# A fixed attention order, wider sums, copied up tiles, five shared PSUM banks and a last tile in halves, in an attention and gated-MLP kernel

## The chip, the cores and the metric

The kernel runs on one core of a Trainium2 chip. The metric is device time in microseconds (us) of one execution; lower is better. "Span" is the time from the first to the last instruction in the trace of one profiled execution, 1.7 to 2.9 us less than the time reported for the same execution.

Engines in the profile: PE is TensorE, PEld its weight loads, DVE is VectorE, ACT is ScalarE, POOL is GpSimd, SP is SyncE; a "q" behind a name is the engine's issuing of DMA transfers.

## The reference

Layer norm of x (2048 rows of 512), then a sliding, dilated attention (32 heads of 16, 8 keys at a distance of 2), times a silu gate from a GELU-gated MLP of width 1792, plus x. All in bfloat16.

```python
def _A_ref(x, wqkv, wo):                      # H = 32, Dh = 16, W = 8, dil = 2
    q, k, v = ...                             # x @ wqkv, by heads
    idx = pos[:, None] - arange(W)[None, :] * dil
    logits = einsum("bhsd,bhswd->bhsw", q, k[idx]) * Dh ** -0.5   # masked where idx < 0
    attn = softmax(logits)
    return einsum("bhsw,bhswd->bhsd", attn, v[idx]) @ wo

def _B_ref(x, w_gate, w_up, w_down):
    return (gelu(x @ w_gate) * (x @ w_up)) @ w_down

xn = layernorm(x)
return x + _A_ref(xn, wqkv, wo) * silu(_B_ref(xn, w_gate, w_up, w_down))
```

## The kernel before

The rows are handled in four blocks of 512. For a block, TensorE makes q, k and v; VectorE multiplies q by shifted k (a "product", 128x2048) and adds pairs of products; TensorE sums over the 16 elements of a head with 32-column matmuls ("logits sum", L_ps); ScalarE takes exp; TensorE sums the weights of the eight keys (sum_ps), VectorE takes the reciprocal (rs), TensorE spreads it back to 128 partitions (b_ps) and ScalarE copies it out (b_sb). Then VectorE multiplies the weights by the values and TensorE sums again ("value sums", O_ps). Gate and up matmuls (g_ps, u_ps) and the output tiles (y_ps, s_ps) fill TensorE's time around this.

The program doesn't write its instructions in the order of the code. Every step is a task with an estimated duration, and a planner simulates the engines and writes each engine's instructions in the order of the simulated starts. Each engine then runs its own list strictly in that order.

```python
MM = 0.216          # the planner's durations, us
PROD = 1.14         # a 128x2048 product or pair addition on VectorE
HMUL = 0.6
ACT1 = 0.62
HOP = 0.2
# ... class Order, in run():
    for t in left:
        s = self.ready(t)              # engine free, inputs done, buffer free
        k = (round(s, 3), t.prio, t.seq)
        if best is None or k < best[0]:
            best = (k, t, s)
```

PSUM has eight banks here: four for q/k/v, gate, up and output tiles, two for the small attention tiles and transposes, and one tile of two banks for the value sums.

```python
psf = pool("psf", 4, space=bass.MemoryType.PSUM)
psa = pool("psa", 2, space=bass.MemoryType.PSUM)
pso = pool("pso", 1, space=bass.MemoryType.PSUM)
```

The logits are summed in two halves of four keys each, eight matmuls a half.

```python
def reduce(w2=w2, prods=prods):
    L = psa.tile([P, TQ], F32, name="L_ps", tag="a")
    for i in range(2):
        for w4 in range(4):
            nc.tensor.matmul(L[32 * w4 : 32 * (w4 + 1), :], lhsT=quad[:],
                             rhs=prods[2 * i][:, w4, :], start=(i == 0), stop=(i == 1))
# ...
s = add("pe", 0.4, sums, deps=[(e, 0.3) for e in exps], prio=-0.4, takes=[("a", ("sum", j))])
r = add("dve", 1.15, recip, deps=[s], prio=-1.5, frees=[("a", ("sum", j))])
b = add("pe", 0.3, spread_back, deps=[r], prio=-0.4, takes=[("a", ("b", j))])
b_ready[j] = add("act", ACT1, b_copy, deps=[b], prio=-0.6, frees=[("a", ("b", j))])
```

The large weights are loaded from ScalarE's list of instructions:

```python
def start(o, i, dep):
    add("act", 0.5, load(o, i), deps=[dep], prio=-3.0)      # load: nc.scalar.dma_start
start(wg_sb[:], ..., copied[2])
start(wu_sb[:], ..., k_ready[1])
for e in range(4):
    start(wo_sb[32 * e : 32 * (e + 1), :, :], v[e], k_ready[2])
start(wd_sb[:], ..., q_ready[3])
```

The last output tile gates its first 384 columns, then the other 128 (`edges = (0, D - P, D)`), behind one silu over all 512.

The softmax here doesn't subtract the row's maximum and nothing guards it: scores larger than these inputs give would overflow.

## Time and profile before

| | before |
|---|---|
| time, median of 6 runs | 230.94 us (230.4 to 231.9) |
| span of the profiled run | 229.0 us |
| first projection matmul | 7.69 us |
| end of the last matmul to the end | 4.4 us |
| VectorE busy | 193.4 us |
| ScalarE busy | 111.1 us |

Between the first and the last matmul TensorE runs at 0.216 us for every 128x512 matmul, with few gaps. Its lines are shown and read in the prediction below.

In a timeline line the columns are: start, duration of the group, engine, source line, operation, output<-input, number of instructions; in brackets the engine's idle time before it and what ended it. Records of a few matmuls can be missing from a trace. A step between the starts of two matmuls that is exactly twice the usual one is such a hole and not a wait, so I read waits from starts together with their releasers. The size of a TensorE wait is the step between two starts less the usual one; that is up to 0.2 us more than the bracket, which starts counting at a modelled end.

### The profile page before, as it was taken

How to read it: one execution, taken by the hardware profiler on the slowest of the kernel's cores; microseconds unless marked ns; L12 is line 12 of the kernel's file. 1: busy time of each engine (PE TensorE's matmuls, PEld its weight loads, DVE VectorE, ACT ScalarE, POOL GpSimd, SP SyncE). 2: the span in 40 equal slices, each digit the busy share in tenths (PEclk: the TensorE clock that was granted, in tenths of full speed). 3: DMA queues.
4: the chain of work that ended last, by engine and by line, in shares of the span. 5: the costliest groups of instructions: out<-in, count | busy, mean ns of one | idle time of the engine just before them, and what ended most of it. 6: DMA issues, size and time to landing. Idle time of an engine off the chain costs nothing.

```text
span 229.0 us, 3272 instructions
## 1 busy us (share of the span) xinstructions
PE 222.1 (97%) x1234; PEld 104.8 (46%) x1234; DVE 193.4 (84%) x270; ACT 111.1 (49%) x167; POOL 28.3 (12%) x67
## 2 busy tenths in 40 slices
PE   7899999999999999999999999999999999999992
PEld 2796554354444444444444444444444344444441
DVE  4899999999999999999999999999759997342322
ACT  3576568477634365464445374434563164334211
POOL 7102930400412000040400002100000000000000
PEclk9999999999999999999999999999999999999999
DMA  5994799599718000054520011900000100000010
GB/s 172 342 384 163 166 207 375 163 296 336 185 32 186 3 0 23 23 141 94 134 54 3 0 46 28 207 0 0 1 3 23 46 24 0 3 0 0 23 46 25
DMA packets 15072, 22.64 MB, mean 99 GB/s; under 512 B 1472, under 2 KB 11984, under 8 KB 15056
## 3 DMA queue, kind: packets, MB, share of 16 engines
q0 software_dynamic: 2592, 8.54, 16.8%
q1 hardware_dynamic: 8592, 7.57, 10.5%
q10 hardware_dynamic: 3872, 6.32, 7.8%
q8 instruction: 9, 0.15, 0.3%
q14 instruction: 7, 0.06, 0.1%
HBM read 18.22 MB, written 4.21 MB: 98 GB/s over the span
## 4 chain that ended last, share of the span: by engine, by line
PE 88%; DMA 9%; DVE 1%; SPq 0%; ACT 0%; ACTq 0%; issue 0%; DVEq 0%
PE g_ps L710 21%; PE u_ps L710 21%; PE y_ps L764 21%; PE qkv_ps L430 12%; DMA wu_sb<-in_B_w_up_dram 7%; PE s_ps L752 6%; DMA wqkv_sb<-in_A_wqkv_dram 3%; PE O_ps L656 2%; PE L_ps L534 1%; PE tr_ps L351 1%; PE sum_ps L588 0%; PE b_ps L606 0%; SPq L196 0%; DVE sg L778 0%; ACT vst L454 0%; DVE sg L785 0%
## 5 line engine op out<-in xcount | busy, mean ns | idle before, releaser
L710 PE MATMUL g_ps<-xnT,wg_sb 128*128 128x512 bf16 x224 | 57.6, 380 | 0.0
L710 PE MATMUL u_ps<-xnT,wu_sb 128*128 128x512 bf16 x224 | 57.6, 380 | 0.0
L720 ACT ACTIVATE gl<-g_ps 128x512 bf16<-128x512 f32 x56 | 33.4, 597 | 48.8 <-PE g_ps L710 48.7
L764 PE MATMUL y_ps<-wd_sb,hT 128*128 128x512 bf16 x224 | 51.3, 380 | 0.0
L727 DVE TENSOR_TENSOR hT<-gl,u_ps 128x512 bf16<-128x512 bf16 x56 | 38.0, 683 | 12.5 <-PE u_ps L710 12.4
L430 PE MATMUL qkv_ps<-xnT,wqkv_sb 128*128 128x512 bf16 (+1 forms) x240 | 43.9, 337 | 1.1 <-DMA wqkv_sb<-in_A_wqkv_dram 0.6
L639 DVE TENSOR_TENSOR pv<-attn,v_arr 128x2048 bf16<-128x2048 bf16 x32 | 38.4, 1219 | 0.1
L517 DVE TENSOR_TENSOR prod<-q_sb,k_sb 128x2048 bf16<-128x2048 bf16 x32 | 38.3, 1219 | 0.0
L710 PEld LDWEIGHTS <-wg_sb 128*128 128x128 bf16 x224 | 21.4, 98 | 27.6 <-issue 2.5
L710 PEld LDWEIGHTS <-wu_sb 128*128 128x128 bf16 x224 | 21.6, 98 | 27.2 <-issue 1.7
L764 PEld LDWEIGHTS <-hT 128*128 128x128 bf16 x224 | 21.5, 98 | 25.7 <-issue 0.4
L430 PEld LDWEIGHTS <-wqkv_sb 128*128 128x128 bf16 x240 | 24.9, 108 | 16.5 <-issue 1.3
L496 POOL DMA_DIRECT2D v_arr<-vT_dram x32 | 18.7, 590 | 100.9 <-DVE pv L639 86.7
L775 ACT ACTIVATE sil<-y_ps 128x512 bf16<-128x512 f32 x16 | 9.6, 597 | 33.2 <-PE y_ps L764 33.1
L778 DVE TENSOR_TENSOR sg<-sil,s_ps 128x512 bf16<-128x512 bf16 (+2 forms) x17 | 11.1, 653 | 11.5 <-PE s_ps L752 7.7
L527 DVE TENSOR_TENSOR prod<-prod 128x2048 bf16<-128x2048 bf16 x16 | 19.5, 1221 | 0.2
L649 DVE TENSOR_TENSOR pv<-pv 128x2048 bf16<-128x2048 bf16 x16 | 19.5, 1220 | 0.2
L752 PE MATMUL s_ps<-wo_sb,o_sb 128*128 128x512 bf16 (+2 forms) x68 | 16.5, 367 | 0.0
L303 DVE BATCH_NORM_STATS2 stats<-x_sb 128x6 f32<-128x512 bf16 x16 | 10.8, 673 | 2.0 <-DMA x_sb<-in_A_x_dram 2.0
L454 ACT ACTIVATE vst<-qkv_ps 128x512 bf16<-128x512 f32 x16 | 9.4, 600 | 6.3 <-PE qkv_ps L430 3.1
L443 ACT ACTIVATE q_sb<-qkv_ps 128x512 bf16<-128x512 f32 x16 | 9.5, 604 | 4.8 <-PE qkv_ps L430 4.8
L449 ACT ACTIVATE k_sb<-qkv_ps 128x512 bf16<-128x512 f32 x16 | 9.2, 598 | 3.9 <-PE qkv_ps L430 3.9
(56 smaller groups left out, 121.1 us busy)
## 6 DMA issues: line engine op xcount, KB each, us to landing
v_arr<-vT_dram POOLq DMA_DIRECT2D x32, 260.0 KB, 5.2
vT_dram<-vst SPq DMA_DIRECT2D x16, 128.0 KB, 6.0
out_dram<-sg SPq DMA_DIRECT2D x15, 128.0 KB, 1.7
wg_sb<-in_B_w_gate_dram ACTq DMA_DIRECT2D x1, 1792.0 KB, 9.3
wu_sb<-in_B_w_up_dram ACTq DMA_DIRECT2D x1, 1792.0 KB, 15.0
wd_sb<-in_B_w_down_dram ACTq DMA_DIRECT2D x1, 1792.0 KB, 10.0
wqkv_sb<-in_A_wqkv_dram SPq DMA_DIRECT2D x3, 512.0 KB, 6.9
x_sb<-in_A_x_dram SPq DMA_DIRECT2D x2, 512.0 KB, 8.9
```

The source lines that it names most:

```text
L430: nc.tensor.matmul(ps[:, i * n : (i + 1) * n], lhsT=wqkv_sb[:, which, ws], rhs=xnT[:, dk, j * TQ + lo : j * TQ + lo + n], start=(dk == 0), ...
L496: nc.gpsimd.dma_start(out=v_arr[32 * w4 : 32 * (w4 + 1), :, :], in_=src)
L517: nc.vector.tensor_tensor(out=prod[:], in0=tiles["q", j][:, c, :].unsqueeze(1).to_broadcast([P, 4, TQ]), in1=kwin, op=ALU.mult,)
L527: nc.vector.tensor_tensor(out=a[:], in0=a[:], in1=b[:], op=ALU.add)
L639: nc.vector.tensor_tensor(out=pv[:], in0=tiles["attn", j][:, w2, :].unsqueeze(1).to_broadcast([P, 4, TQ]), in1=tiles["va", j, half][:, 4 * ...
L649: nc.vector.tensor_tensor(out=a[:], in0=a[:], in1=b[:], op=ALU.add)
L710: nc.tensor.matmul(ps[:], lhsT=w[:, dk, fc * P : (fc + 1) * P], rhs=xnT[:, dk, j * TQ : (j + 1) * TQ], start=(dk == 0), stop=(dk == NC - 1),)
L720: nc.scalar.activation(out=tiles["gl", j, fc][:], in_=tiles["g_ps", j, fc][:], func=AF.Gelu_apprx_tanh)
L727: nc.vector.tensor_tensor(out=tiles["h", j][:, fc, :], in0=tiles["gl", j, fc][:], in1=tiles["u_ps", j, fc][:], op=ALU.mult,)
L752: nc.tensor.matmul(tiles["s", t][:, cs], lhsT=tiles["o", j][:, c, tt * P : (tt + 1) * P], rhs=wo_sb[:, c, cs], start=(c == 0), stop=(c == ...
L764: nc.tensor.matmul(tiles["y", t][:], lhsT=tiles["h", j][:, fc, tt * P : (tt + 1) * P], rhs=wd_sb[:, fc, :], start=(fc == 0), stop=(fc == N ...
L778: nc.vector.tensor_tensor(out=tiles["sg", t][:, cs], in0=tiles["sil", t][:, cs], in1=tiles["s", t][:, cs], op=ALU.mult,)
```

## The change

The intent: give VectorE less to do and TensorE fewer reasons to wait. In its parts:

- The attention batches have a fixed order on VectorE, with the logits of block j+1 ahead of the values of block j.
- The two halves of the logits are summed in one group of 16 matmuls, with one exp over 1024 columns.
- In blocks 0 and 1, ScalarE copies each up tile out of PSUM, so VectorE multiplies from SBUF.
- The query weights come in four loads, on two queues, ahead of the other weights.
- Five PSUM banks are shared by transposes, projections, gate, up and output tiles; one is left for the small attention tiles.
- The last output tile has its y matmuls, silu, gate, addition and store in two halves of 256 columns.
- The products and their sums, which shared six SBUF buffers, get two and five of their own; the normalised inputs get three buffers in place of four.

```diff
+BATCHES = [
+    ("S", 0), ("S", 1), ("V", 0, 0), ("V", 0, 1), ("S", 2), ("V", 1, 0), ("V", 1, 1),
+    ("S", 3), ("V", 2, 0), ("V", 2, 1), ("V", 3, 0), ("V", 3, 1),
+]
+UP_BY_ACT = [(j, fc) for j in range(2) for fc in range(14)]
 ...
-    psf = pool("psf", 4, space=bass.MemoryType.PSUM)
-    psa = pool("psa", 2, space=bass.MemoryType.PSUM)
+    psf = pool("psf", 5, space=bass.MemoryType.PSUM)
+    psa = pool("psa", 1, space=bass.MemoryType.PSUM)
 ...
+    for k in range(NC):
+        eng = nc.sync if k % 2 == 0 else nc.scalar
+        eng.dma_start(
+            out=wqkv_sb[:, 0, k * D : (k + 1) * D], in_=A_wqkv[k * P : (k + 1) * P, 0:D]
+        )
 ...
-    load_wqkv(0)
     load_wqkv(1)
 ...
+    chain = [None]
+    def add_vector(dur, fn, deps, **kw):
+        chain[0] = add("dve", dur, fn, deps=[*deps, chain[0]], prio=1.0, **kw)
+        return chain[0]
 ...
+    def scores_sum(j):
+        L = pso.tile([P, 2, TQ], F32, name="L_ps", tag="o")
+        for w2 in range(2):
+            for i in (1,) if j in FULL else (0, 1):
+                for w4 in range(4):
+                    nc.tensor.matmul(
+                        L[32 * w4 : 32 * (w4 + 1), w2, :], lhsT=quad[:],
+                        rhs=results[("S", j), 2 * w2 + i][:, w4, :],
+                        start=(i == 0 or j in FULL), stop=(i == 1),
                     )
 ...
+        def evacuate():
+            nc.scalar.activation(out=hidden(), in_=tiles["u_ps", j, fc][:], func=AF.Copy)
 ...
-        edges = (0, D) if not split else (0, D - P, D)
-        columns = [slice(a, b) for a, b in zip(edges, edges[1:])]
+        columns = [slice(0, D // 2), slice(D // 2, D)] if split else [slice(0, D)]
 ...
+            ys = [add_y(cs) for cs in columns]
+            ss = add_s()
 ...
+    for batch in BATCHES:
+        attention_batch(*batch)
```

## The prediction

> **What bounds the kernel now.** I read the page first (parts 1, 2 and 4), then busy time by stage, then the order of time at the few places where TensorE loses something.
>
> ```profile
> PE 222.1 (97%) x1234; PEld 104.8 (46%) x1234; DVE 193.4 (84%) x270; ACT 111.1 (49%) x167; POOL 28.3 (12%) x67
> PE   7899999999999999999999999999999999999992
> ...
> PE 88%; DMA 9%; DVE 1%; SPq 0%; ACT 0%; ACTq 0%; issue 0%; DVEq 0%
> ```
>
> PE is busy in every slice but the first and the last. Busy is not yet full speed, so I checked the spacing: in the chain, four 128x512 matmuls take 0.86 us, 0.216 us each. From the first projection matmul (7.68 us) to the end of the last (224.67 us) the stream runs at that spacing; the starts in the trace show 3 to 4 us of larger steps in all. So the time is 7.7 us of start, 217 us of matmuls and 4.4 us of tail, and only what shortens one of the three can help. By stage (the columns are PE, PEld, DVE, ACT, POOL):
>
> ```profile
> 55.64:81.60 25.96, 25.96 (x137) 10.95 (x135) 25.93 (x30) 12.84 (x19) 4.62 (x8) 1.00 0.47 108
> ...
> 209.00:224.67 15.67, 15.65 (x77) 7.18 (x75) 4.02 (x7) 3.56 (x5) 0.00 (x0) 1.00 0.07 25
> 224.67:229.04 4.37, 0.00 (x0) 0.00 (x0) 1.34 (x4) 0.00 (x0) 0.00 (x0) 0.87 0.11 32
> ```
>
> In the first block of gate and up matmuls (first line) VectorE is as full as PE and ScalarE is half empty. Still PE doesn't wait: VectorE keeps up just in time, so relieving it gives no time by itself.
>
> Three places do lose time. First, the column-tiled sums:
>
> ```profile
> 58.07 1.03 PE L710 MATMUL u_ps<-xnT,wu_sb 128*128 128x512 bf16 x4
> 59.02 0.62 PE L656 MATMUL O_ps<-pv,fold 128*32 128x512 bf16 x8
> 59.57 1.04 PE L710 MATMUL g_ps<-xnT,wg_sb 128*128 128x512 bf16 x4
> ```
>
> The next gate matmul would have begun at 58.07 + 4 x 0.216 = 58.93 and begins at 59.57: eight 32-column matmuls cost 0.64 us, two passes of 0.216 (four run side by side) and 0.20 to switch over and back.
>
> Second, a stall at 43 us, where ScalarE stands still for 3 us while it issues loads and waits, so that the four PSUM banks fill:
>
> ```profile
> 42.80 0.62 PE L534 MATMUL L_ps<-prod,quad 128*32 128x512 bf16 x8
> 43.25 1.08 ACT L454 ACTIVATE vst<-qkv_ps 128x512 bf16<-128x512 f32 x2 [3.08 <-DMA wu_sb<-in_B_w_up_dram]
> 43.90 1.89 PE L430 MATMUL qkv_ps<-xnT,wqkv_sb 128*128 128x512 bf16 x8 [0.48 <-ACT vst L454]
> ```
>
> Third, the two ends:
>
> ```profile
> 6.76 0.43 DVE L361 COPY xnT<-tr_ps 128x512 bf16<-128x512 bf16 x1 [0.49 <-PE tr_ps L351]
> 7.68 2.81 PE L430 MATMUL qkv_ps<-xnT,wqkv_sb 128*128 128x256 bf16 x24 [0.63 <-DMA wqkv_sb<-in_A_wqkv_dram]
> ...
> 223.61 1.04 PE L752 MATMUL s_ps<-wo_sb,o_sb 128*128 128x384 bf16 x8
> 223.81 0.60 ACT L775 ACTIVATE sil<-y_ps 128x512 bf16<-128x512 f32 x1 [3.29 <-PE y_ps L764]
> 224.74 0.56 DVE L778 TENSOR_TENSOR sg<-sil,s_ps 128x384 bf16<-128x384 bf16 x1 [2.75 <-PE s_ps L752]
> ```
>
> The transposed input is there at 7.19, the query weights only at 7.65. At the end the gate on the first 384 columns does not start when their four matmuls are done (about 224.4, and silu is done at 224.41) but after all eight, at 224.74: the program orders accesses to one PSUM bank as a whole.
>
> **What the Trainium skill says.** "TensorE: Matmul & The Clock Gate", section "Back-to-back issue gap", gives N/2.4 + 2.5 ns, 216 ns for 512 columns: the trace has 0.216, so the stream is at its floor. "VectorE: DVE Perf Modes", "The perf-mode tier table", has tensor_tensor at half rate when an operand is in PSUM: the trace agrees, 683 ns for hT (u in PSUM) against 424 for the residual add (both in SBUF). "ScalarE: Activation LUTs", "What ACT_TABLE_LOAD costs", gives about 1283 ns; the trace has 1283. "PSUM — Partial Sum Buffer", "PSUM bank collisions raise a hardware error", tells to guard PSUM by bank, not by address; the late gate above is that rule at work.
>
> **The change part by part.**
> - *Logits sums.* The 64 matmuls stay, but come as 4 groups of 16 in place of 8 of 8: 0.20 + 4 x 0.216 = 1.06 us against 2 x 0.64 = 1.28. Gain 4 x 0.2 = 0.8 us, all on the path. The value sums are unchanged.
> - *Query weights in four loads on two queues, ahead of the others.* The first matmul can begin just after 7.19, 0.4 us earlier. But the value weights landed at 3.27 + 8.2 = 11.5 us (issue plus the longest of their three landing times) and are first used at 11.65; they leave a little later now, so part of it is waited for again. I count 0.3.
> - *Five shared banks in place of four.* One bank more holds 0.86 us of matmuls, more than the 0.5 us stall at 43 us. Gain 0.5, if transposes, which now use the same banks, don't take it.
> - *Up tiles of blocks 0 and 1 copied by ScalarE.* VectorE saves 28 x (0.683 - 0.41) = 7.6 us, none on the path. ScalarE gets 28 x 0.60 = 16.8 us. In the first block it holds 12.8 us in 26; with 14 x 0.6 = 8.4 more, and exp of block 1, which now falls here with two more table loads (1.0 + 2 x 1.28 = 3.6), it is near 24 to 25 of 27. Just enough on average, but exp between two table loads keeps ScalarE from both PSUM tiles for 3.6 us, in which PE fills 3.6 / 0.86 = 4.2 banks of five; the gelu table load just before adds 1.28. So a short stall can appear here: 0 to 1 us.
> - *Fixed order, logits a block ahead.* Values of block j now come last before its output tiles. In the kernel before, both logits of block 1 and the values of block 0 were done by 79.6 us, so the amount needed by then is the same 36 products and sums, but half a logits batch of slack is gone. The 3.8 us that VectorE saves per block replaces it. I count 0.3 us, with a tail to 2.
> - *Last tile in halves.* PE work is the same (28 x 0.109 against 14 x 0.216). Silu of half 0 is placed between the first and second seven matmuls of half 1. Both halves lie in one bank, so by the bank rule that silu waits for those seven, and the next seven wait for silu. Matmul to ScalarE about 0.3, silu on 256 columns about 0.385 (from 597 for 512 and 1023 for 1024), and back: an estimated 0.65 us stall. The VectorE end is no shorter: gates and residuals of 256 columns, interpolated from those of 128, 384 and 512, are 2 x (0.42 + 0.29) = 1.42 us, before 0.56 + 0.36 + 0.28 + 0.23 = 1.43. Loss 0.6.
>
> Sum: -0.8 - 0.3 - 0.5 + 0.6, and new stalls of 0.5 = -0.5 us, 230.4.
>
> **The rivals.** (a) *The order works as meant and no new stall appears*, and the halves don't hold each other up: 230.9 - 1.6 = 229.3. For it: VectorE is 100% busy in the middle now, and more slack lets buffers free earlier. Against: PE doesn't wait for it even now. (b) *ScalarE becomes the bound of blocks 0 and 1*: each exp costs PE 1 to 1.5 us, and the hidden tiles come late at the output tiles: 232 to 233. For it: 24 to 25 of 27 us. Against: exp of blocks 2 and 3 can fall among output tiles, where ScalarE is idle about half the time, and four wide exps in place of eight save table loads. (c) *PE waits for the value sums before each block's output tiles*, as the order was fixed with durations for VectorE some 7% shorter than the trace has (1.14 against 1.22): 2 us at up to three blocks, 235. Against: the same shortfall in the kernel before left no PE stall.
>
> **Range and chances.** Even with all gains and no stall the time is near 229, so 2% (226.3) is out of reach unless the PE stream itself shrinks. 2% slower (235.5) takes 5 us of new stalls, rival (c) in full. The range covers rival (a) and most of (b).
>
> **What would show it.** PE's waits: none at 43 us; logits sums in 4 runs of 16 of about 1.1 us; the first projection matmul near 7.3; ScalarE above 85% in the first gate/up block; in the last tile a gap of about 0.6 us between the seventh and eighth matmul of the second half, released by silu; VectorE near 186 us busy. Wrong, if PE waits on value sums at the output tiles or on up-tile copies for more than 2 us, or if the start moves by over 1 us.

## The result, and the profile after

| | before | after |
|---|---|---|
| median of 6 runs, us | 230.94 | 233.01 |
| lowest to highest, us | 230.4 to 231.9 | 232.47 to 233.24 |
| span of the profiled run, us | 229.0 | 231.1 |
| VectorE busy, us | 193.4 | 187.7 |
| ScalarE busy, us | 111.1 | 121.8 |

The ratio of after to before is 1.0081, with a 95% interval of 1.0055 to 1.0107: within 2%, so "same" by that measure, but the interval excludes 1. Ratios here and below are, to within 0.0005, the mean time of one kernel's runs over the mean of the runs of the kernel before from the same rounds, so not quite the ratio of the medians quoted. Executions over 1.5% slower than the fastest of the same kernel are left out of the means. I predicted a gain of 0.5 us; the kernel lost 2.1 us. The 233.01 lies 0.4 us above the range of 228.8 to 232.6.

The page of the changed kernel, parts 1, 2 and 4:

```profile
PE 220.5 (95%) x1224; PEld 106.9 (46%) x1246; DVE 187.7 (81%) x269; ACT 121.8 (53%) x189; POOL 27.8 (12%) x67
...
PE   7999999898999999999999999999999999999991
...
PE 75%; DMA 11%; DVE 8%; ACT 2%; issue 1%; SPq 0%; ACTq 0%; DVEq 0%
```

VectorE has less to do, as meant, and PE has two slices below 90% in the middle, where it had none. The chain that ended last gives the reading: before, it was PE for 88% and VectorE for 1%; now VectorE holds 8% and ScalarE 2%. So TensorE waits for them somewhere. (22 of 1246 matmul records are missing here, so PE's busy time can't be compared to a microsecond.)

The first block of gate and up matmuls, and the time after the last matmul, by stage (window, length, then busy time and instructions of PE, PEld, DVE, ACT, POOL; then the clock, the DMA share and GB/s):

```profile
55.89:83.58 27.69, 27.13 (x155) 11.55 (x157) 27.48 (x36) 22.87 (x35) 4.62 (x8) 1.00 0.46 110
226.29:231.10 4.81, 0.00 (x0) 0.00 (x0) 1.34 (x4) 0.00 (x0) 0.00 (x0) 1.00 0.10 29
```

ScalarE is busy 22.87 of 27.69 us, 83%, where it was half empty. VectorE is as full as before: the window is 1.73 us longer, and with shorter multiplications of the up tiles it holds 20 products and pair additions where it held 17, and block 1's reciprocal. The tail takes 4.81 us in place of 4.37.

The start, in order of time:

```profile
7.34 2.78 PE L446 MATMUL qkv_ps<-xnT,wqkv_sb 128*128 128x256 bf16 x24 [0.28 <-DVE xnT L377]
...
11.69 1.48 PE L446 MATMUL qkv_ps<-xnT,wqkv_sb 128*128 128x256 bf16 x12 [0.24 <-DMA wqkv_sb<-in_A_wqkv_dram]
```

The first projection matmul starts at 7.34, released by the transposed input and no longer by a load. It comes 0.35 us earlier. But at 11.69 TensorE stands still for the value weights; by the starts, 0.41 us are lost there. The early start is given back whole.

Around 43 us, and the softmax scaling of block 0 that follows:

```profile
43.04 1.05 PE L579 MATMUL L_ps<-res,quad 128*32 128x512 bf16 x16
44.24 2.07 ACT L470 ACTIVATE vst<-qkv_ps 128x512 bf16<-128x512 f32 x4 [4.81 <-PE L_ps L579]
44.89 4.48 PE L446 MATMUL qkv_ps<-xnT,wqkv_sb 128*128 128x512 bf16 x19 [0.80 <-ACT vst L470]
...
48.11 1.02 ACT L588 ACTIVATE attn<-L_ps 128x1024 bf16<-128x1024 f32 x1
49.39 0.30 PE L609 MATMUL sum_ps<-attn,fold 128*32 128x128 bf16 x8
50.58 1.23 DVE L540 TENSOR_TENSOR res<-prod 128x2048 bf16<-128x2048 bf16 x1
51.72 0.95 DVE L619 RECIPROCAL rs<-sum_ps 128x128 f32<-128x128 f32 x1
...
53.08 0.38 PE L627 MATMUL b_ps<-rs,spread 128*128 128x128 bf16 x4 [0.66 <-DVE rs L621]
```

Two things are seen. The stall at 43 us has not gone but grown: by the starts from 0.55 to 0.87 us, because ScalarE stands still for 4.81 us (3.08 before). The releaser named in ScalarE's bracket came last, but it is not what held ScalarE up. Its list has four loads of the output weights in front of that copy:

```profile
38.84 5.28 ACTq L871 DMA_DIRECT2D wo_sb<-in_A_wo_dram  x4
```

Three of them are issued by about 40.8 us, the fourth at 43.55. The up weights, issued at 27.59 us, landed 15.94 us later, at 43.53. Before, the up weights were issued at 27.54, landed 14.99 later at 42.53, and the fourth load was issued at 42.56. In both kernels the fourth load goes out directly after the up weights have landed, and the copies stand behind it. The trace's records say why: the fourth load waits for a semaphore (a counter by which one piece of work tells another that it is done) that has the number of the one that the up weights raise when they land. This is so in all 17 traces; the other three loads have other numbers. The stop is 1.73 us longer than before because it begins 0.74 us earlier (39.43, before 40.17: all four loads now stand together in the list) and ends 0.99 us later, with the up weights.

Then a wait of a new kind: the sum of the softmax weights is done at 49.7, but VectorE is in the middle of the products of block 1. Its reciprocal stands in its list behind one more pair addition (50.58) and begins at 51.72. The spread matmul (53.08) is in TensorE's list too early for that. By the starts it costs 0.82 us, and the same for block 1 at 66.67 us another 0.47. The kernel before has no such wait.

The same pair of lines in block 1, shorter:

```profile
66.10 0.95 DVE L619 RECIPROCAL rs<-sum_ps 128x128 f32<-128x128 f32 x1
...
67.36 0.40 PE L627 MATMUL b_ps<-rs,spread 128*128 128x128 bf16 x4 [0.31 <-DVE rs L621]
```

The last tile:

```profile
224.05 0.38 ACT L805 ACTIVATE sil<-y_ps 128x256 bf16<-128x256 f32 x1 [2.56 <-PE y_ps L793]
224.49 0.92 PE L793 MATMUL y_ps<-wd_sb,hT 128*128 128x256 bf16 x7 [0.47 <-ACT sil L805]
...
225.25 1.04 PE L781 MATMUL s_ps<-wo_sb,o_sb 128*128 128x256 bf16 x8
...
226.38 0.42 DVE L808 TENSOR_TENSOR sg<-sil,s_ps 128x256 bf16<-128x256 bf16 x1 [3.41 <-PE s_ps L781]
```

Silu of the first half runs between the matmuls of the second half, and TensorE waits for it, as the prediction had it: the step between the two y matmuls is 0.744 us in place of 0.109. The first gate waits until all eight s matmuls are done.

And one of the four logits groups in the middle:

```profile
98.35 1.05 PE L579 MATMUL L_ps<-res,quad 128*32 128x512 bf16 x16
99.33 1.04 PE L781 MATMUL s_ps<-wo_sb,o_sb 128*128 128x512 bf16 x4
```

By the starts, sixteen column-tiled matmuls that wait for nothing cost 1.07 us of the stream; before, two groups of eight cost 1.28.

The two traces add up so (us, plus is slower; all but the tail from the starts of matmuls):

| where | after less before |
|---|---|
| first projection matmul, 7.69 to 7.34 | -0.35 |
| wait for the value weights at 11.23 | +0.41 |
| stall at 43 us, 0.55 to 0.87 | +0.32 |
| waits for the reciprocal at 52.04 and 66.67 | +1.29 |
| four logits sums, 1.07 in place of 1.28 | -0.84 |
| silu between the y matmuls of the last tile | +0.64 |
| from the last matmul to the end, 4.39 to 4.81 | +0.42 |
| what is left, spread over small steps (the largest, 0.22 at 64 us, a wait for exp of block 1) | +0.21 |
| sum (span 229.0 to 231.1) | +2.10 |

The last term but one is not due to the halves as such. VectorE's last part is as long as it was: the last store is issued 1.53 us after the last matmul in both traces. But from that issue to the end it takes 2.85 us before and 3.31 after. From two traces this could be luck of one launch. Laid side by side, the 17 profiled runs, one of each kernel, fall into groups by how the weights are loaded:

| query weights | output weights issued by | last store, issue to end, us |
|---|---|---|
| four loads | ScalarE | 3.16 to 3.50 in seven runs, the changed kernel among them; 2.56 in a1, whose last store is 32 KB and not 64 |
| four loads | SyncE | 2.60 in all five (a4, d1, e1, h1, h3) |
| one load | ScalarE | 2.83 to 2.85 in all three (before with 32 KB; b1 and h2 with 64 KB) |
| one load | SyncE | 3.21 in the one (b4) |

The grouping was made afterwards, and why an early load should show in the last store, no run here explains. The 0.41 of the value weights does vary between runs with the same loads (below), and the times over six runs are what I go by.

### The profile page after: what moved, and what is told of

The parts are those of the page before. It is cut to its first block, busy times and chain, and to the rows that moved or that the text cites. A ratio compares the mean times of both kernels' runs of the same rounds, so it can differ in the third digit from the quotient of the medians.

```text
span 231.1 us, 3279 instructions
## 1 busy us (share of the span) xinstructions
PE 220.5 (95%) x1224; PEld 106.9 (46%) x1246; DVE 187.7 (81%) x269; ACT 121.8 (53%) x189; POOL 27.8 (12%) x67
## 4 chain that ended last, share of the span: by engine, by line
PE 75%; DMA 11%; DVE 8%; ACT 2%; issue 1%; SPq 0%; ACTq 0%; DVEq 0%
PE y_ps L793 21%; PE g_ps L725 19%; PE u_ps L725 19%; DMA wu_sb<-in_B_w_up_dram 7%; PE qkv_ps L446 6%; PE s_ps L781 6%; DMA wqkv_sb<-in_A_wqkv_dram 3%; DVE prod L552 3%; PE O_ps L682 2%; DVE res L540 2%; DVE prod L663 2%; DMA x_sb<-in_A_x_dram 1%; PE L_ps L579 1%; PE tr_ps L367 1%; DVE rs L619 1%
## 5 line engine op out<-in xcount | busy, mean ns | idle before, releaser
L793 PE MATMUL y_ps<-wd_sb,hT 128*128 128x512 bf16 (+1 forms) x234 | 50.6, 366 | 0.7 <-ACT sil L805 0.5
L540 DVE TENSOR_TENSOR res<-prod 128x2048 bf16<-128x2048 bf16 x32 | 39.1, 1221 | 0.7
L663 DVE TENSOR_TENSOR prod<-attn,v_arr 128x2048 bf16<-128x2048 bf16 x32 | 38.5, 1218 | 0.2
L750 DVE TENSOR_TENSOR hT<-gl,u_ps 128x512 bf16<-128x512 bf16 x28 | 19.1, 684 | 14.1 <-PE u_ps L725 13.1
L805 ACT ACTIVATE sil<-y_ps 128x512 bf16<-128x512 f32 (+1 forms) x17 | 9.7, 572 | 37.1 <-PE y_ps L793 37.1
L808 DVE TENSOR_TENSOR sg<-sil,s_ps 128x512 bf16<-128x512 bf16 (+1 forms) x17 | 11.1, 652 | 17.4 <-PE s_ps L781 13.6
L745 ACT ACTIVATE hT<-u_ps 128x512 bf16<-128x512 f32 x28 | 16.7, 598 | 5.1 <-PE u_ps L725 4.8
L781 PE MATMUL s_ps<-wo_sb,o_sb 128*128 128x512 bf16 (+1 forms) x67 | 16.2, 367 | 0.0
L750 DVE TENSOR_TENSOR hT<-gl,hT 128x512 bf16<-128x512 bf16 x28 | 11.6, 417 | 0.8 <-ACT hT L745 0.5
L691 ACT ACTIVATE o_sb<-O_ps 128x1024 bf16<-128x1024 f32 x8 | 8.2, 1024 | 7.2 <-PE O_ps L682 7.2
```

Of the source, the lines that this page charges most:

```text
L540: nc.vector.tensor_tensor(out=res[:], in0=pair[0][:], in1=pair[1][:], op=ALU.add)
L663: nc.vector.tensor_tensor(out=pr[:], in0=tiles["attn", j][:, w2, :].unsqueeze(1).to_broadcast([P, 4, TQ]), in1=tiles["va", j, half][:, 4 * ...
L745: nc.scalar.activation(out=hidden(), in_=tiles["u_ps", j, fc][:], func=AF.Copy)
L750: nc.vector.tensor_tensor(out=h, in0=tiles["gl", j, fc][:], in1=u, op=ALU.mult)
L781: nc.tensor.matmul(tiles["s", t][:, cs], lhsT=tiles["o", j][:, c, tt * P : (tt + 1) * P], rhs=wo_sb[:, c, cs], start=(c == 0), stop=(c == ...
L793: nc.tensor.matmul(tiles["y", t][:, cs], lhsT=tiles["h", j][:, fc, tt * P : (tt + 1) * P], rhs=wd_sb[:, fc, cs], start=(fc == 0), stop=(fc ...
```

## The experiments

My theory: four separate local causes, none of which is the amount of work on an engine. (1) The tail: both halves in one bank. (2) ScalarE's stop at the loads of the output weights. (3) The reciprocal behind VectorE's products, with TensorE's list too early for it. (4) The start. The main rival: VectorE's list as a whole is too late between 50 and 70 us, so that a wait taken from one place shows up at the next. A second: ScalarE's copies of the up tiles cost the time.

### a1_tail_whole and a2_tail_own_banks: the last tile

a1 takes the last tile back to one silu over 512 columns and a split at 384:

```diff
-        columns = [slice(0, D // 2), slice(D // 2, D)] if split else [slice(0, D)]
+        edges = (0, D) if not split else (0, D - P, D)
+        columns = [slice(a, b) for a, b in zip(edges, edges[1:])]
...
-            ys = [add_y(cs) for cs in columns]
+            ys = [add_y(whole)]
```

> The changed kernel with the last tile computed as before (y whole, s as 384 and 128 columns). Theory: the halves cost 0.64 us of TensorE stall (0.744 us step in place of 0.109) and 0.42 us after the last matmul (4.81 us in place of 4.39), so this is 1.06 us faster than the changed kernel: about 231.95, ratio to before 1.0035. Rival (the halves are harmless, because what follows the stall was waiting anyway): 233.0, ratio 1.008.

a2 keeps the halves and gives each its own PSUM bank:

```diff
-            if cs.start == 0:
-                tiles["s", t] = psf.tile([P, D], F32, name="s_ps", tag="f")
+            tiles["s", t, cs.start] = psf.tile([P, D], F32, name="s_ps", tag="f")
...
-            if lo == 0 and cs.start == 0:
-                tiles["y", t] = psf.tile([P, D], F32, name="y_ps", tag="f")
+            if lo == 0:
+                tiles["y", t, cs.start] = psf.tile([P, D], F32, name="y_ps", tag="f")
```

> The changed kernel, last tile in halves, but each half's y and s in a PSUM bank of its own. Theory (the shared bank makes silu and the second seven matmuls wait for each other): the 0.74 us step goes, and the first gate starts about 0.4 us before the last matmul's end, so the VectorE end is 0.3 to 0.4 us shorter: 1.0 us faster than the changed kernel, about 232.0, and with no stall in the last tile. Rival (splitting itself costs: more small instructions and a larger last store): the stall stays or the gain is below 0.3 us, 232.7 to 233.0.

a1 took 231.42 us (ratio to before 0.9985, 0.9938 to 1.0032); a2 took 231.98 (1.001, 0.9966 to 1.0055). In both the wait in the last tile is gone. In a2 (order of time):

```profile
224.28 1.04 PE L780 MATMUL s_ps<-wo_sb,o_sb 128*128 128x256 bf16 x8
...
224.97 0.42 DVE L807 TENSOR_TENSOR sg<-sil,s_ps 128x256 bf16<-128x256 bf16 x1 [2.35 <-PE s_ps L780]
```

The first gate now starts at 224.97, before the last s matmul ends (225.32). So the 0.64 us is the shared bank. That halves with two banks beat the old whole tile is not shown: a1 is 0.55 us faster than a2 in the mean. In the profiled runs a2's last store is issued 0.44 us sooner after the last matmul (1.09 us, a1 1.53), but takes 3.16 us to the end where a1's, half as large, takes 2.56. Other differences mix in: in a1's trace the wait for the value weights is absent, and its stall at 43 us was 1.25 us, longer than in the changed kernel by 0.38. The two waits for the reciprocal are 0.82 and 0.47 or 0.48 in both, the same to a hundredth. They come from the order, not from luck.

### b1_before_halves: the same halves on the kernel before

```diff
-        edges = (0, D) if not split else (0, D - P, D)
+        columns = [slice(0, D // 2), slice(D // 2, D)] if split else [slice(0, D)]
...
-            y = add_y()
+            ys = [add_y(cs) for cs in columns]
```

> The kernel before with the changed kernel's last tile in halves (one bank). Theory: the 0.64 us stall appears in the last tile here too, and the end after the last matmul is the same or up to 0.4 us longer: 0.6 to 1.0 us slower than before, 231.5 to 231.9, ratio 1.003 to 1.0045. Rival: no difference.

It took 231.92 us beside 231.15 for the kernel before: ratio 1.0041 (1.0008 to 1.0075), 0.95 us. The trace has the same 0.64 us between y matmuls, at 222.88. (Its first projection matmul started at 7.34, with the query weights in one load; this matters in h2 below.) This part of the change costs time by itself, whatever the rest does.

### a3_vector_times: the planner is told VectorE's true durations

```diff
-PROD = 1.14
-HMUL = 0.6
-HMUL2 = 0.34
+PROD = 1.22
+HMUL = 0.69
+HMUL2 = 0.42
```

(Also the other VectorE durations: statistics, normalisation, the transposes' copies, the reciprocal.)

> The changed kernel with the order planned with the VectorE durations that the trace shows (product 1.22, hT 0.69 and 0.42, statistics 0.86, normalise 0.42, copy 0.42, reciprocal 1.20), no other edit. Theory A (the order puts the spreading matmuls b_ps before VectorE can have the reciprocal, because it was planned with VectorE 7% too fast): TensorE's two waits on b_ps (0.82 and 0.47 us) shrink below 0.2 us each, 231.7 to 232.0. Theory B (the first of them comes from ScalarE standing still for 4.8 us at 39 to 44 us, which no VectorE duration cures): only the 0.47 goes, 232.5. Either way the stall at 43 us stays.

It took 240.09 us, ratio 1.0358 (1.0304 to 1.0413). The waits for the reciprocal did go, to 0.12 us at most. But every engine's list changed. The logits sum of block 0 came at 48.12 us in place of 43.04, and its waits of TensorE (line waited for: total us, times, longest) now begin with

```profile
PE O_ps L682 <- DVE res L540: 3.2, 1, 3.2
```

for a value sum; the stall at 43 us grew to 2.0 us, and after the long wait the granted clock was 0.50 from 85.9 to 92 us. Both theories had given numbers for this run, and both missed. Correct durations in a planner of this kind don't give a good order by themselves, since they move everything; I could not use this run to settle the cause and went over to edits that move one instruction at a time.

### a4_wo_on_sync: the output weights loaded from SyncE

```diff
-        def load(o, i):
-            return lambda: nc.scalar.dma_start(out=o, in_=i)
+        def load(o, i, q):
+            return lambda: q.dma_start(out=o, in_=i)
...
-            start(wo_sb[32 * e : 32 * (e + 1), :, :], v[e], k_ready[2])
+            start(wo_sb[32 * e : 32 * (e + 1), :, :], v[e], k_ready[2], nc.sync)
```

The order on PE, DVE and POOL is the same as in the changed kernel; only these four loads change hands.

> The changed kernel with the four wo loads issued by SyncE in place of ScalarE; the order on the four compute engines is the same. Theory B (ScalarE stands still because the fourth wo load isn't issued until the up weights have landed): ScalarE's idle of 4.8 us at 39 to 44 us goes, so the stall of 0.87 us at 43 us goes, exp of block 0 starts near 44.5 in place of 48.1, and the first wait on b_ps (0.82 us) goes: about 1.6 us faster, 231.4. Theory A: the stall at 43 us goes (0.87) but the waits on b_ps stay: 232.1. A third way: the load is held back on SyncE too, v stores behind it are late, ScalarE waits for their buffers instead: no gain, 233.

It took 231.17 us, ratio 0.9981 (0.9937 to 1.0025), 1.84 us less than the changed kernel. In order of time:

```profile
42.62 1.05 PE L579 MATMUL L_ps<-res,quad 128*32 128x512 bf16 x16
43.60 4.51 PE L446 MATMUL qkv_ps<-xnT,wqkv_sb 128*128 128x512 bf16 x19
...
51.65 0.38 PE L627 MATMUL b_ps<-rs,spread 128*128 128x128 bf16 x4 [0.60 <-DVE rs L621]
```

The projection follows the logits sum without a wait, so cause (2) is shown: 0.87 us, by the loads in ScalarE's list. SyncE's fourth load again went out only at 43.13, right after the up weights (issued 27.17, landed 15.95 us later), but now nobody who matters stands behind it. In spans the gain is 2.1 us: 0.87 here, 0.41 from a wait for the value weights that didn't occur in this run, and 0.71 from a last store that ended sooner. The first is the change's own. The last goes with it too, by the table above, without a known reason; the 0.41 may be chance.

The run tells one thing more. Exp of block 0 came 2.3 us earlier than in the changed kernel (45.83), the sum at 48.04, and the wait at the spread matmul is still 0.76 us. VectorE's one idle stretch there, 1.00 us at 48.2 in the changed kernel, waiting for this exp, is gone as well. Earlier input doesn't help: the reciprocal stands behind VectorE's products in its list.

### c1_spread_one_later: the spread matmul one piece later in TensorE's list

```diff
         def b_copy():
-            tiles["b", j] = atpool.tile([P, TQ], BF16, name="b_sb", tag="b_sb")
+            spread_back(); tiles["b", j] = atpool.tile([P, TQ], BF16, name="b_sb", tag="b_sb")
...
-        b = add("pe", 0.3, spread_back, deps=[r], prio=-0.4, takes=[("a", ("b", j))])
+        b = add("pe", 0.3, lambda: None, deps=[r], prio=-0.4, takes=[("a", ("b", j))])
```

The planner's timing stays as it was, but the matmuls are written when their reader is, one piece of the main stream later. Only TensorE's order differs.

> The changed kernel with the four spreading matmuls b_ps put one piece (usually four matmuls, 0.86 us) later in TensorE's order; the order on the other engines is the same. Theory (the two waits on b_ps, 0.82 and 0.47 us, are TensorE reaching them before the reciprocal, and are worth their length): both fall below 0.15 us, 1.2 us faster than the changed kernel, about 231.8. Rival (what is saved there is waited for later, because VectorE is behind): 232.6 to 233.0, with new waits on O_ps or hT.

It took 233.08 us, ratio 1.0077 (1.0052 to 1.0101): nothing gained. The waits at the spread are gone, and another is there:

```profile
58.86 1.23 DVE L540 TENSOR_TENSOR res<-prod 128x2048 bf16<-128x2048 bf16 x1
60.14 0.40 PE L579 MATMUL L_ps<-res,quad 128*32 128x512 bf16 x4 [0.73 <-DVE res L540]
```

TensorE now waits 0.90 us for the last pair of block 1's logits, and 0.29 for a value sum: 1.19 us by the starts, for the 1.29 that went. The rival was right here, and cause (3) as I had put it was too narrow: VectorE is late throughout this stretch, and a wait removed at one place is taken at the next.

### a5_up_by_vector: without ScalarE's copies

```diff
-UP_BY_ACT = [(j, fc) for j in range(2) for fc in range(14)]
+UP_BY_ACT = []
```

> The changed kernel with no up tile copied by ScalarE (VectorE multiplies from PSUM in all blocks, as before). Theory (the copies give TensorE nothing, as it doesn't wait for VectorE; but with the fixed order VectorE must finish block 0's values by the output tiles): if the copies pay, VectorE's extra 0.27 us x 14 = 3.8 us per block makes TensorE wait on O_ps or s_ps at 80 us: 235 or more. If they are idle, 233.0 as with them. If they hurt (ScalarE as a bound), 232 or less.

It took 235.2 us, ratio 1.0167 (1.0137 to 1.0197), 2.2 us above the changed kernel. By the starts, the waits for the reciprocal grew from 1.29 us in two to 2.02 in three, and there were new ones of 0.75 at 83.8 us (an output tile waits for o_sb) and of 0.74 at 100 us (logits). So the copies aren't the cost; under the fixed order they are needed. The second rival falls.

### f1_four_banks: four shared banks and two small ones

```diff
-    psf = pool("psf", 5, space=bass.MemoryType.PSUM)
-    psa = pool("psa", 1, space=bass.MemoryType.PSUM)
+    psf = pool("psf", 4, space=bass.MemoryType.PSUM)
+    psa = pool("psa", 2, space=bass.MemoryType.PSUM)
```

> The changed kernel with four shared banks and two for the small sums, in place of five and one. If the fifth bank works as I predicted (0.86 us of matmuls that can go on while ScalarE stands still): the stall at 43 us grows from 0.87 to about 1.7 us, and around the exp of block 1 (60 to 64 us) TensorE waits up to 1 us for a bank: 233.9 to 235, ratio 1.012 to 1.017. If the bank is worth nothing: 233.0.

It took 234.52 us, ratio 1.0177 (1.0131 to 1.0223). The wait of TensorE at 43 us, in the view of waits:

```profile
PE qkv_ps L446 <- ACT vst L470: 1.6, 1, 1.6
```

By the starts it is 1.74 us against 0.87. The fifth bank is worth 0.87 us at this place, one bank's worth of matmuls (4 x 0.216 = 0.86). It did what I had said of it; the stop of ScalarE that it was to bridge grew by more.

### g1_no_look_ahead: the fixed order without the block ahead

```diff
-    ("S", 0), ("S", 1), ("V", 0, 0), ("V", 0, 1), ("S", 2), ("V", 1, 0), ("V", 1, 1),
-    ("S", 3), ("V", 2, 0), ("V", 2, 1), ("V", 3, 0), ("V", 3, 1),
+    ("S", 0), ("V", 0, 0), ("V", 0, 1), ("S", 1), ("V", 1, 0), ("V", 1, 1), ("S", 2),
+    ("V", 2, 0), ("V", 2, 1), ("S", 3), ("V", 3, 0), ("V", 3, 1),
```

> The changed kernel with each block's values straight after its logits (S0 V0 S1 V1 ...), no logits a block ahead. If looking ahead is what keeps VectorE working through the softmax chain (exp to normalise takes 48.1 to 60.0 us for block 0 in the trace, of which 6 us are needed), VectorE idles some 5 us per block and the values of later blocks come late at their output tiles: 235 to 240, with VectorE waiting for b_sb. If the order costs more than it gives: 231 to 233, with no waits on b_ps.

It took 238.63 us, ratio 1.0317 (1.0289 to 1.0345). The spread matmuls don't wait, since VectorE itself now stands waiting for the softmax sums:

```profile
DVE rs L619 <- PE sum_ps L609: 13.8, 4, 5.3
```

That is 13.8 us in four waits of an engine that must work for most of the span. So this fixed order needs its block of look-ahead. The price is that the logits of block 1 have to be complete before the values of block 0 begin.

### d1_three_mended, e1_sums_later_too and h3_spread_two_later: all that was found, together

d1 is a2, a4 and c1 in one kernel. e1 also writes the logits and value sums one piece later:

```diff
         def expo():
-            tiles["attn", j] = atpool.tile([P, 2, TQ], BF16, name="attn", tag="attn")
+            scores_sum(j); tiles["attn", j] = atpool.tile([P, 2, TQ], BF16, name="attn", tag="attn")
...
         def evacuate():
+            values_sum(j, half)
...
-            "pe", 0.21 + MM * len(res), lambda: scores_sum(j) if kind == "S" else values_sum(j, half),
+            "pe", 0.21 + MM * len(res), lambda: None,
```

h3 also moves the spread by another piece:

```diff
-        b_ready[j] = add("act", ACT1, b_copy, deps=[b], prio=-0.6, frees=[("a", ("b", j))])
+        b_ready[j] = add("act", ACT1, b_copy, deps=[(b, 1.0)], prio=-0.6, frees=[("a", ("b", j))])
```

> The changed kernel with three mends together: a bank of its own for each half of the last tile, wo loads issued by SyncE, b_ps one piece later. If the three costs are independent: 233.0 - 1.0 - 1.5 - 1.2 = 229.3, ratio 0.993, no TensorE wait over 0.2 us after 12 us. If one hides another: 230.0 to 230.8.

> d1 (the three mends) with the logits sums L_ps and the value sums O_ps also put one piece later in TensorE's order, other engines' order as in d1. Theory (VectorE is up to 0.8 us behind the plan at 58 to 69 us and catches up by itself, so room of one piece at each sum is enough): the waits of 0.66 and 0.18 us go, nothing new before the first s_ps: span 227.4, time 229.3, 0.8 us faster than d1. Rival (VectorE's lag is passed on, as in c1): a wait of 0.4 us or more at O_ps, hT or s_ps takes their place, 229.9 to 230.3.

> e1 with b_ps one piece later still. If the remaining 0.38 us wait on b_ps is worth its length: 0.3 us faster than e1, 229.5, ratio 0.993. If VectorE's lag is passed on again: the wait turns up at O_ps or s_ps and the time is e1's, 229.8.

| kernel | median, us | ratio to before (95%) | waits of TensorE that remain in the middle |
|---|---|---|---|
| d1 | 230.10 | 0.9962 (0.9931 to 0.9992) | 0.77 logits at 58.1, 0.28 value sum |
| e1 | 229.84 | 0.9945 (0.9913 to 0.9977) | 0.38 spread at 65.86 |
| h3 | 229.06 | 0.9911 (0.9882 to 0.9939) | none over 0.1 |

With each step the last wait in the middle moves or shrinks, and in h3 it is gone. Its page, parts 1 and 4:

```profile
PE 220.3 (97%) x1246; PEld 106.7 (47%) x1246; DVE 187.5 (83%) x269; ACT 120.3 (53%) x189; POOL 28.3 (12%) x67
...
PE 95%; DVE 2%; DMA 1%; issue 0%; DVEq 0%
```

All matmul records are there, and the chain that ended last is PE for 95%, more than in either kernel before it. All that TensorE waits for, by the view of waits, lies in the first 8 us:

```profile
PE warm_ps L301 <- DVE eps_sb L239: 1.2, 1, 1.2
PE tr_ps L367 <- DVE xn_t L351: 1.2, 1, 1.2
PE qkv_ps L446 <- DVE xnT L377: 0.3, 1, 0.3
```

VectorE is as busy as in the changed kernel (187.5 and 187.7), so less work on it isn't what mended this. TensorE's list gives it more room at all three places where the two meet. h3 is the fastest kernel, 0.9% below the kernel before.

### b4_before_mended and h1_before_all_but_attention: is the attention part worth it?

b4 is the kernel before with the output weights on SyncE and the halves in their own banks (edits as in a4 and a2). h1 adds the four loads of the query weights (edit as in the change), so it has everything of h3 that doesn't touch the attention order, its sums, the copies or the shared banks.

> The kernel before with the wo loads issued by SyncE and the last tile in halves with a bank each; attention as before. Theory: its stall of 0.55 us at 43 us goes and the VectorE end is 0.45 us shorter: 1.0 us faster than before, about 230.0, ratio 0.9957. If then the kernel d1 (0.9962) is not faster than this, the changed attention part gives nothing over the old one. Rival: the stall was hidden by something after it, ratio 0.998.

> b4 (the kernel before, wo loads by SyncE, halves of the last tile with a bank each) with the query weights in four loads as in the change; attention, banks and up tiles as before. First projection matmul at 7.34 in place of 7.7 to 8.4 us: 0.3 to 0.7 us faster than b4, ratio 0.9965 to 0.998. If the changed attention part gives its 0.8 us of merged sums, e1 (0.9945) stays ahead by 0.3 to 0.8 us; if all its gain is lost to VectorE's lag, this one is as fast as e1.

b4 took 230.83 us, ratio 0.9994 (0.9963 to 1.0026). Its stall at 43 us is gone, but in the profiled run the first projection matmul came only at 8.35, as the query weights were late. h1 took 229.85, ratio 0.9934 (0.9912 to 0.9956), with no wait over 0.2 us after the first 12 us. Against h3's 0.9911 (0.9882 to 0.9939) the intervals overlap. But h1 and h3 ran in the same call and can be compared directly: the mean times are 229.82 and 229.18, and the six spans lie between 227.6 and 228.5 for h1 and between 226.8 and 227.7 for h3, 0.9 us apart in the mean. So the attention part of the change, once mended, probably gives 0.6 to 0.9 us, about the 0.8 of the merged sums; in the times alone the difference is at the edge of the noise. Some 70% of what h3 gained over the kernel before can be had with three small edits to the kernel before.

### h2_query_weights_one_load: the start alone

The changed kernel with the query weights in one load, as before:

```diff
-    for k in range(NC):
-        eng = nc.sync if k % 2 == 0 else nc.scalar
-        eng.dma_start(
-            out=wqkv_sb[:, 0, k * D : (k + 1) * D], in_=A_wqkv[k * P : (k + 1) * P, 0:D]
-        )
...
+    load_wqkv(0)
     load_wqkv(1)
```

> The changed kernel with the query weights in one load on SyncE's queue as before; nothing else. Theory (the four loads bring the start forward, and part of it is waited for again on the value weights): first projection matmul at 7.6 to 8.4 us in place of 7.34, wait for the value weights near 11.2 us gone: 0 to 0.6 us slower than the changed kernel, 233.0 to 233.6. Rival (the loads on ScalarE's queue delay its table load and the start is worse for it): 232.6.

It took 231.94 us, ratio 1.0047 (1.0006 to 1.0089), an interval that overlaps that of the changed kernel (1.0055 to 1.0107). Its six spans scatter from 229.3 to 232.3, those of the changed kernel from 230.8 to 231.3. In the profiled run, the shortest of the six, the first projection matmul started at 7.36 all the same, nothing waited for the value weights, and there was no stall at 43 us. So in the changed kernel I can't say from the times what the four loads are worth. (The two longest of the six have a granted clock of 0.988 and 0.989, the others 0.995 or more.) In the kernel before (h1 against b4, sent in different calls) they go with a gain of 0.6%.

The profiled runs, laid side by side, show more. With four loads the first projection matmul starts between 7.33 and 7.54 in twelve runs and at 6.94 in a3; with one load at 7.34 (b1), 7.36 (h2), 7.69 (before) and 8.35 (b4). So the four loads don't make the best start earlier, they avoid the late ones. And the up weights, issued near 27 us, took 15.0 to 15.5 us to land in the four runs with one load, and 15.6 to 16.3 in twelve of the thirteen with four (15.05 in f1). The span of h2's profiled run is 1.80 us shorter than the changed kernel's, and 1.75 of it lies in three places: no stall at 43 us (0.87), no wait for the value weights (0.41), and a last store of 2.84 us (0.47). This makes the four loads a rival cause of the later up weights, and through them of the larger stall at 43 us. It is a lead from single profiles, not a result.

## Why the prediction was wrong

The class with the highest chance was the right one, 0.92 for a change within 2%. The time was off by 2.6 us, and the range missed by 0.4. The 2.6 in the terms below: start 0.36, banks 0.82, new stalls 0.79, last tile 0.04, tail 0.42, the small rest 0.21, less 0.04 for the logits sums. Four steps failed: the gain from the fifth bank, the slack of the fixed order, the size of what the start gives back, and the tail taken as unchanged. By its own steps:

- **Logits sums, -0.8.** Right. A group of 16 costs 1.07 us by the starts, predicted 1.06.
- **Query weights in four loads, -0.3.** Mechanism right, size wrong. The first matmul came 0.35 us earlier, and the term "part of it is waited for again" was put at about 0.1 and measured 0.41 in the profiled run. Net +0.06. The wait for the key or value weights differs from run to run: 0.16 to 0.60 us in nine of the thirteen profiled runs with the four loads, absent in a1, a4, a5 and h3.
- **Five shared banks, -0.5.** This step failed. The bank holds 0.87 us of matmuls, as said (f1). But I took ScalarE's stop of 3.08 us as given, though its cause, a load that isn't issued until another has landed, stood in the line that I showed (`<-DMA wu_sb`). The stop grew to 4.81 (0.74 us by the place of the loads in the list, 0.99 by the later up weights), and the stall from 0.55 to 0.87. Size of the error: 0.8 us. What was to be removed was the load from ScalarE's list (a4), not bridged.
- **Up tiles copied by ScalarE, "none on the path".** VectorE fell to 187.7, predicted near 186. ScalarE was 83% busy in the first block, I had said above 85%. No bank wait showed near exp, so the 0 to 1 us stall set aside for that didn't occur. But "none on the path" was wrong for the new order: without the copies it is 2.2 us slower (a5).
- **Fixed order, +0.3, in the sum part of the 0.5 for new stalls.** This step failed: the new stalls are 1.29. I counted the products needed before the output tiles, and asked about slack only there. Waits came earlier, where the short chain exp, sum, reciprocal, spread crosses VectorE's products: 0.82 and 0.47. I had even noted that the planner's durations for VectorE are 7% short, in rival (c), and dismissed it because the kernel before has the same shortfall and no stall. It has another order; its VectorE isn't behind when the softmax chain asks for it. The size of the error is about 0.8 us.
- **Last tile in halves, +0.6.** Right in mechanism and size: 0.64, and the trace has silu as the releaser. With the kernel before it is the same (b1), and with two banks it goes (a2).
- **The tail after the last matmul** I predicted as unchanged, and this failed. VectorE's part is as predicted (1.53 us to the last store in both). The last store took about 0.45 us longer, in this kernel as in the six others with the same loads and a 64 KB last store. The cause is open.

Of the rivals, (b) fell: ScalarE is no bound. The 233 that it gave is near the measured time for another reason. (c) was the right place to look, TensorE early for a late VectorE, but it named the value sums before the output tiles and got the wrong wait.

What is shown: the shared bank in the last tile (a1, a2, b1); the loads in ScalarE's list at 43 us (a4); that VectorE's lag between 50 and 70 us passes from wait to wait (c1, d1, e1) and ends when TensorE's list gives room at all three (h3). What is argued only: that the lag comes from having to complete the logits of block 1 before the values of block 0. g1 shows that the look-ahead can't simply be left out, but not that it makes the lag. The SBUF buffers of the products and sums, changed together with the order, are a rival for it that no run separates. Why the fourth load waits for the up weights is in the records: the two share a semaphore. What stays open: why the up weights land nearly 1 us later and the last store takes longer in the changed kernel (the four query loads go with both), and how much of the start's gain is real.

## What to carry to other kernels

When engines run fixed lists, ask of every short chain that crosses a busy engine where it stands in that engine's list, and not only whether the engine has time in sum. A removed wait counts as gained only when the trace shows the next one didn't take it; move one instruction at a time in one engine's list to see that. Work split in halves needs a bank for each half, and a load that may have to wait belongs in the list of an engine on which nothing urgent stands behind it.

## What the Trainium skill lacked or had wrong

- "TensorEngine Tiling (Array Packing)", section "Key Properties": it says that changing the tiling mode drains TensorE, and the traces fit it, but it gives no size. Here a switch to 32 columns and back costs about 0.20 us: 8 matmuls take 0.64 and 16 take 1.07, where four side by side take 0.206 to 0.217.
- "DMA: Bandwidth & Descriptors", section "Issuing engines are not separate DMA queues": it says that issuing from several engines saves only the time on the sequencer, which is "usually small". That sentence leaves out what an issue may wait for. In the changed kernel ScalarE took 2.5 us to issue four loads and stood 2.75 us more before the fourth, until the up weights had landed; the same four loads from SyncE took 0.87 us of wait off TensorE. The wait is this program's and not the chip's: the two loads share a semaphore (landed 43.53, issued 43.55; before 42.53 and 42.56).
- "TensorE: Matmul & The Clock Gate", section "Back-to-back issue gap": it calls the 216 ns the gap of an isolated matmul and gives about 131 ns a matmul for 512 columns as the sustained rate of a real kernel. In the traces before and after no gate, up or output matmul of 512 columns is followed by its next in less than 215 ns.
- "PSUM — Partial Sum Buffer", section "PSUM bank collisions raise a hardware error": its rule to guard by bank has a price that it doesn't give. Two halves of a tile in one bank cost 0.64 us of TensorE here, with two banks none.
